# Float32 score and fold products as 64x32 tiles on a pair of PSUM banks, two conversion steps on GpSimd

## Chip, core and metric

The kernel runs on one core of a Trainium2 chip. The metric is the device time of one execution in microseconds (us), lower is better. PE is TensorE (PEld its weight loads), DVE is VectorE, ACT is ScalarE, POOL is GpSimd; SP only issues transfers. A matmul multiplies a stationary operand (`lhsT`, up to 128 rows by 128 columns) with a moving one (`rhs`) into PSUM, which has eight banks of 512 float32 columns in each of 128 partitions. A product that uses only 64 or 32 of the stationary columns writes only as many partitions, and another product can use the other columns at the same time. A float32 product stands in the profile as two MATMUL rows, a float16 product as one.

## What is computed

Eight batches of eight heads: attention over 32 memory slots that are made from k, v and phi, and then a feed-forward layer on all 4608 tokens, with g = h cos(h).

```python
def _attn_ref(q, k, v, phi):
    a = np.exp(phi - np.max(phi, axis=2, keepdims=True))
    a = a / (np.sum(a, axis=2, keepdims=True) + 1e-09)
    k_m = np.einsum('bhsm,bhsd->bhmd', a, k)
    v_m = np.einsum('bhsm,bhsd->bhmd', a, v)
    scores = scale * np.matmul(q, k_m.transpose(0, 1, 3, 2))
    attn = np.exp(scores - np.max(scores, axis=-1, keepdims=True))
    attn = attn / (np.sum(attn, axis=-1, keepdims=True) + 1e-09)
    return np.matmul(attn, v_m)

h = x @ w_in          # x: (4608, 512), the attention's output; w_in: (512, 2048)
g = h * np.cos(h)
return g @ w_out      # w_out: (2048, 512)
```

The shapes are 8 batches, 8 heads, 576 positions, head size 64, 32 slots. The weights arrive as 64-bit floats.

## The kernel before

**Folding.** The attention's last product and the layer's first are both linear, so the kernel multiplies v_m with w_in once for each batch (the *fold*, 256 x 2048) and then takes h as attn times the fold. Batch 0 folds in float32 (`fold_first`, eight pieces of 256 columns), batch 1 in float32 as well (`fold`, four pieces q of 512 columns); batches 2 to 7 fold in float16 pairs, a high and a low part.

**Groups.** The 4608 tokens are taken as 12 groups of 384. A group has 16 steps f, one for each 128 of the 2048 hidden columns: `gemm1` makes h (tile `hp`), `act` and `act_end` make g on ACT and DVE, `gemm2` adds g times w_out to three accumulators (`acc`), four steps behind. Group 0 works in float32, the others in float16 pairs. Step f of `gemm2` reads `wo[:, f + 1]`.

**Conversion.** w_in comes in eight pieces (in0 to in7), w_out in eight (out0 to out7), each as 1024 pairs of 32-bit words in every partition. `to_float32` makes float32 of them: DVE writes the sign into the upper 16 bits (line 143), ACT writes the first bits below it (147), ACT scales the high words in place (151), DVE joins them (152), ACT squares for the later scale (154). The pieces follow in the order out0, in2, in3, out1, out2, in4, in5, out3, out4, in6, in7, out5, out6, out7, one in each step of group 0 (`convert_next`); in0 and in1 come ahead of it. Piece out j becomes `wo[2j+1]` and `wo[2j+2]`, so step f = 12 needs out6 and f = 14 needs out7. Raw words lie in three rotating buffers (`raw0` to `raw2`), in2 and in3 in free parts of `wo`; the next load into a buffer waits for the square. When in7 and out7 are done, `weight_scale` takes a maximum over all partitions with a GpSimd all-reduce (line 178), and all float16 parts of the weights need its result.

**Attention of a batch.** `memory` makes k_m and v_m (`psA`, then a transposing product into `tpx`), and copies them into `km` and `vm`, 64 columns for a pair of heads: the two heads lie in the two halves of the rows and of the columns, and GpSimd sets the rest to zero. Another all-reduce (line 312) gives v's scale. `attend` makes the scores in blocks of 256, 256 and 64 positions, transposes them on DVE in 32 x 32 squares, takes the softmax and transposes back. It is a generator, 24 steps long, that the main loop runs a few steps at a time beside the groups of the batches ahead of it.

**Order.** Each engine has one queue, worked off in order. A scheduler sets the order from the written one; the line behind a wait waits too. Scores, folds and other small products share two PSUM banks that rotate (`small_ps`).

Of the kernel before, what the change touches and what calls it, by code (L numbers as in the profile page):

```python
# [45 lines left out]
def attention_then_ffn(ctx: ExitStack, tc: tile.TileContext, phi, phiT, kv, qT, w_in, w_out, eye, out):  # L46
# [86 lines left out]

    def to_float32(dst, raw, sq_to, pin=False, after_sign=None):
# [8 lines left out]
        sign = nc.vector.tensor_scalar(out=halves[:, :, :, 1], in0=high_top, scalar1=0.0, scalar2=-32768.0,  # L143
                                       op0=ALU.is_lt, op1=ALU.mult)
# [2 lines left out]
        begin = nc.scalar.activation(halves[:, :, :, 0], low_top, AF.Copy, scale=2.0 ** -5, bias=-31.0 / 64.0)
# [3 lines left out]
        nc.scalar.activation(high.bitcast(F32), high.bitcast(F32), AF.Copy, scale=2.0 ** -112)
        nc.vector.scalar_tensor_tensor(out=dst.bitcast(I32), in0=high, scalar=3, in1=dst.bitcast(I32),
                                       op0=ALU.logical_shift_left, op1=ALU.bitwise_or)
        nc.scalar.activation(low.bitcast(F32), dst, AF.Square, accum_out=sq_to)

    def convert_w_in(j, after_sign=None):
        to_float32(w_in_sb[:, :, j * WS:(j + 1) * WS], loads.pop(("in", j)), sq[:, 0, j:j + 1], j == 1, after_sign)

# [68 lines left out]
    def memory(b):  # L227
# [65 lines left out]
        km = wk.tile([P, NP, 2 * M], F32, tag="km", name=f"km_{b}", bufs=1)
        vm = wk.tile([P, NP, 2 * M], F32, tag="vm", name=f"vm_{b}")
        nc.gpsimd.memset(km, 0.0)
        nc.gpsimd.memset(vm, 0.0)
# [52 lines left out]
    def attend(b):  # L349
# [18 lines left out]

        sc_at = {}

        def score_products(i):
            t0, n = BL[i]
            sc_at[i] = sc = small_ps(f"sc_{b}_{t0}")
            for g in range(2):
                for p in range(2):
                    nc.tensor.matmul(sc[D * p:D * (p + 1), g * n:(g + 1) * n], lhsT=km[:, 2 * g + p],  # L376
                                     rhs=qt[:, 2 * g + p, t0:t0 + n], start=True, stop=True)
# [37 lines left out]
        if b == 0:  # L415
            for p in ((0, 1), (2,)):
                for i in p:
                    scores(i)
                if p[0] == 0:
# [9 lines left out]
        score_products(0)
        score_products(1)  # L430
        score_back(0)
        score_back(1)
# [27 lines left out]
    def fold_psum(b, q, g):  # L460
        pv = small_ps(f"pv_{b}_{q}_{g}")
        for i in range(2):
            c = 2 * g + i
            if b < 2:
                nc.tensor.matmul(pv[D * i:D * (i + 1)], lhsT=st["vm", b][:, c],
                                 rhs=w_in_sb[:, c, q * FS:(q + 1) * FS], start=True, stop=True)
        if b >= 2:
            for first in (True, False):
                for j in range(4):
                    c, o = 2 * g + j // 2, 1 - j % 2  # L470
                    nc.tensor.matmul(pv[M * j:M * (j + 1)], lhsT=(st["vp", b] if first else vl)[:, c, o],  # L471
                                     rhs=st["w2", q][:, c, o], start=first, stop=not first, skip_group_check=True)
# [8 lines left out]
    def fold(b, q):  # L481
        vw = wk.tile([P, 2, 2, FS], F16, tag="vw", name=f"vw_{b}_{q}", bufs=8)
        st["vw", b, q] = vw
        for g, pv in enumerate([fold_psum(b, q, g) for g in range(2)]):
            split_fold(b, vw, g, pv)

    def fold_first(j):
        q, r = divmod(j, 2)
# [2 lines left out]
        pv = small_ps(f"pvf_{j}").rearrange("p (g x) -> p g x", g=2)
        for g in range(2):
            for i in range(2):
                c = 2 * g + i
                nc.tensor.matmul(pv[D * i:D * (i + 1), g], lhsT=st["vm", 0][:, c],
                                 rhs=w_in_sb[:, c, j * WS:(j + 1) * WS], start=True, stop=True)
# [299 lines left out]
```

## Time and profile before

| what | value |
|---|---|
| median of 2 runs | 709.72 us (709.52 to 709.92) |
| the profiled execution | 710.08 us, its span 708.3 us |
| busy: PE, DVE, ACT, POOL | 97%, 75%, 73%, 2% of the span |
| first product of group 0's `gemm2` | at 41.6 us |
| group 1 opens (first L577) | at 125.2 us |
| mean granted TensorE clock | 0.994 of full speed |

Busy time of PE is that of its rows, which are pipelined, so a busy PE need not be PE at its peak. Releasers (behind `<-`) are inferred from semaphores.

```profile
PE   8699899999999999999999999999999999999997
DVE  3889879999968966599667886599567976575552
ACT  1899999897985865778666875778766875665652
POOL 0000000000000000000000100000000000000000
DMA  8996782326407100160105200160100000100101
PE acc L577 33%; PE hp L533 16%; DVE u L547 4%; ACT u L552 3%; DVE u L556 3%; DVE gp L559 3%; PE psA L270 3%; DVE vw L478 2%; PE sc L376 2%; PE pv L471 2%; ACT gp L558 2%; DMA phi<-in_phi 2%; DVE wo L191 2%; PE hp L524 1%; DVE w_in_parts L202 1%
```

The first five lines cut the span into 40 slices of 17.7 us; a digit is the busy share in tenths. The last line is the chain of work that ended last, its share of the span by line: half of it is the two large products, L577 and L533.

### The profile page before, as it was taken

The page shows a single profiled execution, that of the slowest core. Times are in us where ns is not written, and L with a number is a line of the kernel's source. Part 1 is how long each engine was busy: PE and PEld are TensorE (multiplying, and loading weights), DVE is VectorE, ACT ScalarE, POOL GpSimd, SP SyncE. Part 2 cuts the span into 40 slices and gives each one's busy share as a digit, 9 for nine tenths or more (in the row PEclk, how much of TensorE's full clock was granted, in tenths as well). Part 3 has the DMA queues.
Part 4 walks back from the last instruction along what each step waited for, and adds up shares of the span by engine and source line. Part 5 has one row for each costly group of instructions (what it writes and reads, how often), then busy time and mean ns, then how long its engine had stood idle before and what let it go on. Part 6 is the DMA issues. An engine that isn't in the chain of part 4 may idle for free.

```text
span 708.3 us, 11822 instructions
## 1 busy us (share of the span) xinstructions
PE 687.8 (97%) x4597; PEld 364.7 (51%) x4597; DVE 532.7 (75%) x1135; ACT 518.7 (73%) x951; POOL 13.7 (2%) x34
## 2 busy tenths in 40 slices
PE   8699899999999999999999999999999999999997
PEld 3354345565555445666445445666445454665553
DVE  3889879999968966599667886599567976575552
ACT  1899999897985865778666875778766875665652
POOL 0000000000000000000000100000000000000000
PEclk9999999999999999999999999999999999999999
DMA  8996782326407100160105200160100000100101
GB/s 281 379 321 218 266 293 60 105 61 195 146 1 237 44 1 1 56 226 1 44 1 167 99 16 1 46 206 31 44 2 2 22 23 1 46 1 1 45 1 44
DMA packets 31959, 66.18 MB, mean 93 GB/s; under 512 B 2208, under 2 KB 12320, under 8 KB 31904
## 3 DMA queue, kind: packets, MB, share of 16 engines
q1 hardware_dynamic: 27440, 57.43, 25.0%
q10 hardware_dynamic: 4464, 8.00, 3.0%
q8 instruction: 36, 0.59, 0.3%
q14 instruction: 19, 0.16, 0.1%
HBM read 51.79 MB, written 9.44 MB: 86 GB/s over the span
## 4 chain that ended last, share of the span: by engine, by line
PE 60%; DVE 21%; ACT 16%; DMA 2%; issue 1%; ACTq 0%; POOL 0%; DVEq 0%; SPq 0%
PE acc L577 33%; PE hp L533 16%; DVE u L547 4%; ACT u L552 3%; DVE u L556 3%; DVE gp L559 3%; PE psA L270 3%; DVE vw L478 2%; PE sc L376 2%; PE pv L471 2%; ACT gp L558 2%; DMA phi<-in_phi 2%; DVE wo L191 2%; PE hp L524 1%; DVE w_in_parts L202 1%
## 5 line engine op out<-in xcount | busy, mean ns | idle before, releaser
L577 PE MATMUL acc<-wo,gp 128*128 128x512 f16 x1584 | 371.8, 379 | 1.2 <-DVE ob L589 0.7
L577 PEld LDWEIGHTS <-gp 128*128 128x128 f16 x1584 | 153.3, 98 | 162.6 <-issue 4.1
L533 PE MATMUL hp<-aT,vw 128*128 128x192 f16 (+1 forms) x1440 | 202.7, 284 | 1.0 <-DVE u L556 1.0
L533 PEld LDWEIGHTS <-vw 128*128 128x128 f16 x1440 | 128.3, 98 | 77.4 <-issue 17.5
L552 ACT ACTIVATE u<-u,quarter 128x384 f32<-128x384 f32 x192 | 116.7, 615 | 63.8 <-DVE u L547 62.9
L556 DVE SCALAR_TENSOR_TENSOR u<-hp,u 128x384 f32<-128x384 f32 x176 | 96.5, 553 | 60.6 <-ACT u L552 60.1
L544 ACT ACTIVATE gp<-hp,cu 128x192 int32<-128x192 f32 (+1 forms) x240 | 115.4, 492 | 28.1 <-PE hp L533 12.3
L547 DVE SCALAR_TENSOR_TENSOR u<-hp,cu,gp 128x192 f32<-128x192 f32 (+1 forms) x240 | 118.8, 503 | 21.9 <-ACT gp L544 21.5
L559 DVE TENSOR_TENSOR gp<-u,gp 128x384 f16<-128x384 f32 x176 | 96.4, 552 | 43.0 <-ACT gp L558 41.9
L558 ACT CAST gp<-u 128x384 f16<-128x384 f32 x176 | 88.8, 510 | 54.3 <-DVE u L556 53.0
L572 PE MATMUL acc<-wo,gp 128*128 128x512 f32 x96 | 45.1, 599 | 0.0
L478 DVE SCALAR_TENSOR_TENSOR vw<-pv,vw 128x512 f16<-128x512 f32 x48 | 31.5, 684 | 3.0 <-ACT vw L477 2.9
L524 PE MATMUL hp<-aT,vf 128*128 128x384 f32 x64 | 25.6, 533 | 7.9 <-DVE vf L497 3.1
L477 ACT ACTIVATE vw<-pv 128x512 f16<-128x512 f32 x48 | 26.8, 589 | 1.1 <-PE pv L471 0.9
L572 PEld LDWEIGHTS acc<-wo,gp 128*128 128x128 f32 x96 | 17.4, 190 | 17.8 <-issue 15.2
L601 ACT ACTIVATE ob<-acc,os 128x512 f32<-128x512 f32 x27 | 17.8, 682 | 9.6 <-PE acc L577 7.1
L524 PEld LDWEIGHTS hp<-aT,vf 128*128 128x128 f32 x64 | 12.2, 202 | 20.1 <-issue 4.3
L552 ACT ACT_TABLE_LOAD x17 | 21.8, 1283 | 0.3
L270 PE MATMUL psA<-kv,phi 128*32 128x129 f32 (+1 forms) x640 | 21.0, 275 | 0.7 <-ACT phi L260 0.5
L376 PE MATMUL sc<-q,km 128*64 128x256 f32 (+3 forms) x192 | 19.8, 342 | 1.6 <-DVE vw L478 1.2
L270 PEld LDWEIGHTS psA<-kv,phi 128*32 128x32 f32 (+1 forms) x640 | 16.4, 109 | 7.3 <-issue 3.3
L376 PEld LDWEIGHTS sc<-q,km 128*64 128x64 f32 x192 | 12.1, 140 | 12.0 <-issue 3.6
(136 smaller groups left out, 544.7 us busy)
## 6 DMA issues: line engine op xcount, KB each, us to landing
kv<-in_kv SPq DMA_DIRECT2D x32, 516.0 KB, 6.9
raw_out<-in_w_out SPq DMA_DIRECT2D x8, 1024.0 KB, 5.8
q<-in_qT SPq DMA_DIRECT2D x7, 1152.0 KB, 6.0
out<-ob ACTq DMA_DIRECT2D x30, 256.0 KB, 2.1
raw_in<-in_w_in SPq DMA_DIRECT2D x6, 1024.0 KB, 8.1
phi<-in_phi SPq DMA_DIRECT2D x8, 512.0 KB, 5.9
w_in_sb<-w_in_parts SPq DMA_DIRECT2D x12, 256.0 KB, 4.0
kv<-in_kv SPq DMA_DIRECT2D x8, 258.0 KB, 8.5
```

The lines of the kernel that those rows point to most:

```text
L270: nc.tensor.matmul(psA[32 * j:32 * (j + 1), g * KV:(g + 1) * KV], lhsT=a[:n, c, h * M:(h + 1) * M], rhs=kvs[c][:n, h * KV:(h + 1) * KV], s ...
L376: nc.tensor.matmul(sc[D * p:D * (p + 1), g * n:(g + 1) * n], lhsT=km[:, 2 * g + p], rhs=qt[:, 2 * g + p, t0:t0 + n], start=True, stop=True)
L478: nc.vector.scalar_tensor_tensor(out=vw[:, 1, g], in0=src, scalar=T, in1=vw[:, 0, g], op0=ALU.mult, op1=ALU.subtract)
L533: nc.tensor.matmul(hp[:, c0:c0 + n], lhsT=vw[:, wi, g, fo * P:(fo + 1) * P], rhs=aT[:, ai, g, c1:c1 + n], start=(k == 0), stop=(k == 5))
L544: ins = nc.scalar.activation(ni[:, c], hp[:, c], AF.Copy, scale=cu, bias=0.25)
L547: nc.vector.scalar_tensor_tensor(out=u[:, c], in0=hp[:, c], scalar=cu, in1=ni[:, c], op0=ALU.mult, op1=ALU.subtract)
L552: nc.scalar.activation(u, u, AF.Sin, scale=TWO_PI_BELOW, bias=quarter)
L556: nc.vector.scalar_tensor_tensor(out=u, in0=hp[:, :GT], scalar=2.0 ** -17, in1=u, op0=ALU.mult, op1=ALU.mult)
L558: nc.scalar.copy(gp[:, 0], u)
L559: nc.vector.tensor_tensor(out=gp[:, 1], in0=u, in1=gp[:, 0], op=ALU.subtract)
L572: nc.tensor.matmul(accs[grp][t], lhsT=gp[:, t * P:(t + 1) * P], rhs=wo[:, f + 1], start=(f == 0), stop=(f == NF - 1))
L577: nc.tensor.matmul(accs[grp][t], lhsT=gp[:, gi, t * P:(t + 1) * P], rhs=parts[:, wi], start=(f == 0 and gi == 0 and wi == 0), stop=(f == N ...
```

## The change

**Tiles.** `km` and `vm` lose their zero halves: 32 columns for a pair of heads, the even head's 64 rows over the odd head's (for `vm` the other way round). A score product now takes 64 rows and 32 columns, one head, and the head's half g goes to bank g of a pair of banks; column quarter c takes pair c. A block is eight products. The float32 folds are cut the same way (`fold_single`); the float16 folds keep their shape. Scores come in two blocks of 288 positions instead of 256, 256 and 64 (batch 0: 384 and 192). The two banks that rotated are now one tile, `pair`, whose halves are handed out in turn.

**Conversion.** For all pieces but in0 and in1 the sign goes from DVE to GpSimd and the scaling from ACT to GpSimd. Each is a TENSOR_SCALAR over 1024 columns. GpSimd's memsets of `km` and `vm` are gone.

```diff
@@ attention_then_ffn
+    ps_s = ctx.enter_context(tc.tile_pool(name="ps_s", bufs=1, space=PSUM))
+    pair = ps_s.tile([P, 2, 512], F32, name="pair")
+    turn = itertools.count()
     def small_ps(name):
-        return ps_s.tile([P, 512], F32, tag="ps_s", name=name)
+        return pair[:, next(turn) % 2]
@@ to_float32
-        sign = nc.vector.tensor_scalar(out=halves[:, :, :, 1], in0=high_top, scalar1=0.0, scalar2=-32768.0,
-                                       op0=ALU.is_lt, op1=ALU.mult)
+        sign = (nc.vector if early else nc.gpsimd).tensor_scalar(out=halves[:, :, :, 1], in0=high_top, scalar1=0.0, scalar2=-32768.0,
+                                                                        op0=ALU.is_lt, op1=ALU.mult)
...
-        nc.scalar.activation(high.bitcast(F32), high.bitcast(F32), AF.Copy, scale=2.0 ** -112)
+        if early:
+            nc.scalar.activation(high.bitcast(F32), high.bitcast(F32), AF.Copy, scale=2.0 ** -112)
+        else:
+            nc.gpsimd.tensor_scalar(out=high.bitcast(F32), in0=high.bitcast(F32), scalar1=2.0 ** -112, scalar2=None,
+                                    op0=ALU.mult)
@@ memory
-        nc.gpsimd.memset(km, 0.0)
-        nc.gpsimd.memset(vm, 0.0)
...
-        nc.scalar.mul(km[lo, :, 0:M], tv[lo, :, 0], 1.0 / math.sqrt(D))
+        nc.scalar.mul(km[lo], tv[lo, :, 0], 1.0 / math.sqrt(D))
@@ attend
         def score_products(i):
             t0, n = BL[i]
-            sc_at[i] = sc = small_ps(f"sc_{b}_{t0}")
-            for g in range(2):
-                for p in range(2):
-                    nc.tensor.matmul(sc[D * p:D * (p + 1), g * n:(g + 1) * n], lhsT=km[:, 2 * g + p],
-                                     rhs=qt[:, 2 * g + p, t0:t0 + n], start=True, stop=True)
+            for c in range(NP):
+                for g in range(2):
+                    rows = slice(g * D, (g + 1) * D)
+                    nc.tensor.matmul(pair[M * c:M * (c + 1), g, :n], lhsT=km[rows, c],
+                                     rhs=qt[rows, c, t0:t0 + n], start=True, stop=True)
 
         def score_back(i):
             t0, n = BL[i]
-            nc.vector.transpose(at[:, 2 * t0:2 * (t0 + n)], sc_at[i][:, :2 * n])
+            for g in range(2):
+                nc.vector.transpose(at[:, 2 * t0 + g * n:2 * t0 + (g + 1) * n], pair[:, g, :n])
@@ after fold_psum
+    def fold_single(b, c0, n):
+        for c in range(NP):
+            for g in range(2):
+                rows = slice((1 - g) * D, (2 - g) * D)
+                nc.tensor.matmul(pair[M * c:M * (c + 1), g, :n], lhsT=st["vm", b][rows, c],
+                                 rhs=w_in_sb[rows, c, c0:c0 + n], start=True, stop=True)
```

Lines of the changed program are numbered anew: the sign is line 145, the scaling 156, the joining 158, scores 378, the all-reduces 184, 229 and 316.

POOL's queue up to the third batch, before (an ISA row with a name is an all-reduce, one without a name has no operands and stands ahead of an instruction of another kind; `km` and `vm` are set to zero):

```order
L296 MEMSET vm_480 128x256
L312 ISA
L312 ISA l_0_235<-l_0_233 128x1
L295 MEMSET km_479 128x256
L312 ISA l_1_492<-l_1_490 128x1
L295 MEMSET km_1587 128x256
L296 MEMSET vm_1588 128x256
L178 ISA m_in<-m_in 128x1
L178 ISA m_out<-m_out 128x1
```

The same queue now, from out2 to in5's scaling (`raw_out_324` is out2, `raw_in_328` and `raw_in_344` are in4 and in5, `l_1` is v's scale of batch 1):

```order
L145 TENSOR_SCALAR wo<-raw_out_324 128x1024
L156 TENSOR_SCALAR raw_out_324<-raw_out_324 128x1024
L316 ISA
L316 ISA l_1_494<-l_1_492 128x1
L145 ISA
L145 TENSOR_SCALAR w_in_sb<-raw_in_328 128x4x256
L145 TENSOR_SCALAR w_in_sb<-raw_in_344 128x4x256
L156 TENSOR_SCALAR raw_in_328<-raw_in_328 128x1024
L156 TENSOR_SCALAR raw_in_344<-raw_in_344 128x1024
```

The memsets are gone, two TENSOR_SCALAR rows stand for each piece, and a row without operands stands wherever the queue goes between an all-reduce and a TENSOR_SCALAR.

The end of the conversions on the same queue now (`raw_out_588` is out5, `raw_out_625` out6, `raw_out_648` out7):

```order
L156 TENSOR_SCALAR raw_out_588<-raw_out_588 128x1024
L184 ISA
L184 ISA m_in<-m_in 128x1
L145 ISA
L145 TENSOR_SCALAR wo<-raw_out_625 128x1024
L145 TENSOR_SCALAR wo<-raw_out_648 128x1024
L156 TENSOR_SCALAR raw_out_625<-raw_out_625 128x1024
L156 TENSOR_SCALAR raw_out_648<-raw_out_648 128x1024
L184 ISA
L184 ISA m_out<-m_out 128x1
```

The all-reduce for w_in's scale now stands between out5 and out6, and both signs stand ahead of both scalings.

PE's queue at the scores of batch 4, before (`sc_0` and `sc_256` are its first two blocks, `gp_4` is step 4 of a group) and then now:

```order
L577 MATMUL acc_0_2923<-wo,gp_4_2914 128x512
L376 MATMUL sc_0_3139<-q_2223,km_3062 64x256 x4
L376 MATMUL sc_256_3144<-q_2223,km_3062 64x256 x4
L577 LDWEIGHTS gp_4_2914
L577 MATMUL acc_0_2923<-wo,gp_4_2914 128x512
```

```order
L572 MATMUL acc_0_2915<-wo,gp_5_2981 128x512
L378 MATMUL pair<-q_2229,km_3052 32x288 x8
L572 LDWEIGHTS gp_5_2981
L572 MATMUL acc_0_2915<-wo,gp_5_2981 128x512
L572 LDWEIGHTS gp_5_2981
```

Eight products of 64 rows, 32 columns and 288 positions stand where eight of 128 rows, 64 columns and 256 positions stood; the second block of eight follows some rows later, where the third block of four small products stood.

More of the change, by code (lines that the diff above doesn't have):

```diff
@@ L156, in convert_w_in @@
     def convert_w_in(j, after_sign=None):
[L157 removed]
+        to_float32(w_in_sb[:, :, j * WS:(j + 1) * WS], loads.pop(("in", j)), sq[:, 0, j:j + 1], j == 1, after_sign, j < 2)
     def convert_w_out(j):
@@ L292, in memory @@
             nc.tensor.matmul(tpx[:, g * P:(g + 1) * P], lhsT=X[:, g], rhs=ident, start=True, stop=True)
[L293 to L296, printed above, removed]
+        km = wk.tile([P, NP, M], F32, tag="km", name=f"km_{b}", bufs=1)
+        vm = wk.tile([P, NP, M], F32, tag="vm", name=f"vm_{b}")
         tv = tpx[:, 0:HM].rearrange("p (c t m) -> p c t m", t=2, m=M)
         lo, hi = slice(0, D), slice(D, P)
-        nc.scalar.mul(km[lo, :, 0:M], tv[lo, :, 0], 1.0 / math.sqrt(D))
-        nc.scalar.mul(km[hi, :, M:2 * M], tv[hi, :, 1], 1.0 / math.sqrt(D))
-        nc.vector.tensor_copy(out=vm[hi, :, 0:M], in_=tv[hi, :, 0])
-        nc.vector.tensor_copy(out=vm[lo, :, M:2 * M], in_=tv[lo, :, 1])
+        nc.scalar.mul(km[lo], tv[lo, :, 0], 1.0 / math.sqrt(D))
+        nc.scalar.mul(km[hi], tv[hi, :, 1], 1.0 / math.sqrt(D))
+        nc.vector.tensor_copy(out=vm[hi], in_=tv[hi, :, 0])
+        nc.vector.tensor_copy(out=vm[lo], in_=tv[lo, :, 1])
         st["km", b], st["vm", b] = km, vm
@@ L415, in attend @@
         if b == 0:
[L416 to L419, printed above, removed]
+            for i in range(2):
+                p = (i,)
+                scores(i)
+                if i == 0:
                     yield
@@ L424, in attend @@
                 normalize(p)
-                for i in p:
-                    back(i)
+                back(i)
                 yield
             return
[L429 to L432, printed above, removed]
+        scores(0)
         yield
-        score_products(2)
-        score_back(2)
+        scores(1)
         yield
@@ L438, in attend @@
             load_q(b + 1)
-        pieces = ((0,), (1, 2))
+        pieces = ((0,), (1,))
         for p in pieces:
@@ L453, in attend @@
         yield
+        yield
         back(1)
         yield
-        back(2)
-        yield
     def fold_psum(b, q, g):
[L461 to L472, printed above, removed]
-        return pv
+        pv = pair[:, g]
+        for first in (True, False):
+            for c in range(NP):
+                nc.tensor.matmul(pv[M * c:M * (c + 1)], lhsT=(st["vp", b] if first else vl)[:, c, 1 - g],
+                                 rhs=st["w2", q][:, c, 1 - g], start=first, stop=not first, skip_group_check=True)
+        return pv
+    def fold_single(b, c0, n):
+        for c in range(NP):
+            for g in range(2):
+                rows = slice((1 - g) * D, (2 - g) * D)
+                nc.tensor.matmul(pair[M * c:M * (c + 1), g, :n], lhsT=st["vm", b][rows, c],
+                                 rhs=w_in_sb[rows, c, c0:c0 + n], start=True, stop=True)
     def split_fold(b, vw, g, src):
@@ L483, in fold @@
         st["vw", b, q] = vw
-        for g, pv in enumerate([fold_psum(b, q, g) for g in range(2)]):
-            split_fold(b, vw, g, pv)
+        if b < 2:
+            fold_single(b, q * FS, FS)
+        for g in range(2):
+            split_fold(b, vw, g, fold_psum(b, q, g) if b >= 2 else pair[:, g])
     def fold_first(j):
@@ L490, in fold_first @@
             st["vf", q] = wk.tile([P, 2, FS], F32, tag="vw", name=f"vf_{q}", bufs=8)
[L491 to L496, printed above, removed]
+        fold_single(0, j * WS, WS)
+        pv = pair[:, :, 0:WS]
         (nc.scalar.copy if j < 2 else nc.any.tensor_copy)(out=st["vf", q][:, :, r * WS:(r + 1) * WS], in_=pv)
```

10 lines of the change are left out of this document (4 added, 6 removed).

## The prediction

> **What bounds the kernel now.** I read the busy sums of six stretches first, to learn which engine is full where.
>
> ```profile
> 20.00:41.60 21.60, 14.63 (x63) 6.85 (x61) 16.96 (x24) 20.09 (x27) 0.00 (x0) 0.92 1.05 359
> 41.60:83.40 41.80, 38.66 (x207) 19.25 (x206) 38.08 (x75) 39.27 (x57) 0.98 (x3) 0.96 0.77 267
> 83.40:125.20 41.80, 41.80 (x169) 20.58 (x168) 36.71 (x82) 41.60 (x71) 1.02 (x3) 1.00 0.56 178
> 183.40:708.30 524.90, 518.25 (x3588) 276.89 (x3585) 376.05 (x805) 362.21 (x693) 9.38 (x17) 1.00 0.15 50
> ```
>
> The columns are length, then busy time of PE, PEld, DVE, ACT and POOL, the granted clock, DMA share and GB/s. From 183 us on PE is busy for 518.25 of 524.90 us: there the end moves by what PE is relieved of. Until 125 us, where group 0 runs and the weights are converted, ACT is full (41.60 of 41.80), and POOL does next to nothing (1.02). Second, the timeline of the stretch in which conversion ends, to see what waits for it.
>
> ```profile
> 97.42 2.74 PE L572 MATMUL acc<-wo,gp 128*128 128x512 f32 x6
> 100.00 1.45 PE L524 MATMUL hp<-aT,vf 128*128 128x384 f32 x4
> 101.28 2.74 PE L572 MATMUL acc<-wo,gp 128*128 128x512 f32 x6
> 108.86 2.77 PE L572 MATMUL acc<-wo,gp 128*128 128x512 f32 x6
> 111.56 1.94 PE L465 MATMUL pv<-w_in_sb,vm 128*64 128x512 f32 x8
> 125.21 0.81 PE L577 MATMUL acc<-wo,gp 128*128 128x512 f16 x3
> ...
> 97.91 1.23 DVE L152 SCALAR_TENSOR_TENSOR wo<-raw_out,wo 128x1024 int32<-128x1024 int32 x1 [0.46 <-ACT raw_out L151]
> 104.05 1.23 DVE L152 SCALAR_TENSOR_TENSOR wo<-raw_out,wo 128x1024 int32<-128x1024 int32 x1 [0.21 <-ACT raw_out L151]
> ```
>
> The L572 rows at 97.42, 101.28 and 108.86 are f = 9, 10 and 12 of group 0; L577 at 125.21 opens group 1. Step f = 12 reads what out6 became, and that was ready at 99.14 (97.91 + 1.23), out7 at 105.28. So conversion now leads its reader by about 10 us.
>
> **The change, part by part.** *Conversion.* Fourteen of the sixteen conversions (all but in0 and in1) hand the sign to POOL instead of DVE, and the scaling to POOL instead of ACT.
>
> ```profile
> L143 DVE TENSOR_SCALAR wo<-raw_out 128x1024 int16<-128x1024 int8 x8 | 6.0, 751 | 0.0
> L151 ACT ACTIVATE raw_out<-raw_out 128x1024 f32<-128x1024 f32 x8 | 9.2, 1147 | 0.0
> L154 ACT ACTIVATE raw_out<-wo 128x1024 f32<-128x1024 f32 x8 | 9.3, 1161 | 0.0
> L223 POOL PARTITION_ALL_REDUCE mx<-mx x4 | 5.1, 1278 | 22.9 <-DVE mx L222 11.8 <-DVE rs L395 11.1
> L296 POOL MEMSET vm<- 128x256 f32 x8 | 2.4, 312 | 134.8 <-DVE vl L343 53.6 <-PE pv L465 36.3 <-PE pvf L495 31.2
> 222.34 1.07 POOL L223 PARTITION_ALL_REDUCE mx<-mx  x1 [4.73 <-DVE mx L222]
> ```
>
> Off DVE go 14 x 0.75 = 10.5 us, off ACT 14 x 1.15 = 16.1 us. On POOL come 28 instructions over 1024 columns, and the trace has none like them. The lower end is the memset, which only writes: 0.312 us for 256 columns, at most 1.25 us for 1024. The upper end is the all-reduce, which reads, computes and writes 256 columns: 1.07 us in a single row, 1.28 in the mean of four, so 4.3 to 5.1 us for 1024. A scaling reads, computes and writes, and the sign does two operations and writes 2-byte pieces 4 bytes apart: I hold them nearest to the all-reduce and take 4.7 us, 9.4 us for a conversion. Conversions now come every 5.2 us (83.6 us of group 0 in 16 steps), so POOL becomes the engine on which group 0 waits, and what DVE and ACT save buys nothing.
>
> *Code on POOL.* In the changed program's POOL order, five unnamed ISA rows stand ahead of out6: each time POOL goes between the all-reduce and TENSOR_SCALAR. Before, that row stands once, ahead of the first all-reduce, and the profile knows it by another name:
>
> ```profile
> L312 POOLq MODIFY_POOL_CONFIG  x2: 13/13/13, 1.6 to 1.6; - x2
> 17.30 0.35 POOL L312 PARTITION_ALL_REDUCE l<-l  x1 [15.76 <-DVE l L310]
> L552 ACT ACT_TABLE_LOAD x17 | 21.8, 1283 | 0.3
> ```
>
> Issued at 1.6, first used at 17.30: such a switch of code costs between nothing and 15.7 us. ACT's table load, 1.28 us, is the only other row in which an engine changes what it runs, and it fetches a table, not code; no row settles it, so I take the middle of the ends, 7.8. The Trainium skill (GPSIMD Engine Reference, Instruction dispatch) gives about 6 us for the first call after such a load, which no run here shows yet; by it the five come to 30 us in place of 39, and my time would be 9 us lower.
>
> *The sum on POOL.* POOL is free at 17.65 (17.30 + 0.35). Ahead of out6's last scaling lie 12 conversions and three of the four instructions of out6 and out7 (both signs stand first): 13.5 x 9.4 = 126.9 us. Add five switches, 39.0, and two all-reduces, 0.7.
>
> One stall comes on top. Out1's scaling waits for ACT's first step on out1, and that stands on ACT behind in3's square, which waits through DVE for POOL's scaling of in3.
>
> ```profile
> 41.26 1.13 ACT L154 ACTIVATE wo<-w_in_sb 128x1024 f32<-128x1024 f32 x1
> 49.86 1.39 ACT L147 ACTIVATE wo<-raw_out 128x1024 int16<-128x1024 uint8 x1
> ```
>
> From the square's end (42.39) to that step ACT needs 7.5 us; with the step itself 8.9. Ahead go DVE's 1.23 and the square's 1.13, and POOL covers 4.7 with out1's sign: 11.3 - 4.7, some 6.6 us of stall. Then DVE's last step on out6, 1.2. In all 17.65 + 126.9 + 39.0 + 0.7 + 6.6 + 1.2 = 192.1 us, where step f = 12 could start at 108.86: 83.2 us later. Two things could come later still, and don't.
>
> ```profile
> 107.23 0.35 POOL L178 PARTITION_ALL_REDUCE m_out<-m_out  x1 [14.07 <-DVE m_out L177]
> 111.59 0.77 ACT L190 ACTIVATE wo<-wo,s_out 128x512 f16<-128x512 f32 x1
> ...
> raw_out<-in_w_out SPq DMA_DIRECT2D x8, 1024.0 KB, 5.8
> ```
>
> Group 1 also needs w_out's scale: out7's scaling, a sixth switch, the all-reduce and the 4.0 us that now lie between it and the first split (107.58 to 111.59) make 4.7 + 7.8 + 0.4 + 4.0 = 16.9 us behind out6's last scaling; step 12's own way to group 1 takes 1.2 + 16.4 (125.21 - 108.86). And three raw buffers rotate, so a load has about two conversions, 19 us, against 5.8 us to landing.
>
> *Scores.* Six batches (2 to 7) have theirs in the part that PE bounds.
>
> ```profile
> 308.07 1.95 PE L376 MATMUL sc<-q,km 128*64 128x256 f32 x16
> 309.95 1.90 PE L577 MATMUL acc<-wo,gp 128*128 128x512 f16 x8
> 311.78 0.45 PE L376 MATMUL sc<-q,km 128*64 128x64 f32 x8
> 312.16 1.17 PE L533 MATMUL hp<-aT,vw 128*128 128x192 f16 x12
> ...
> 48.19 2.54 PE L270 MATMUL psA<-kv,phi 128*32 128x129 f32 x80
> ```
>
> PE goes on 1.88 us after the first, 0.38 after the second: 2.26 a batch. The 16 rows (a float32 product is two) went in pairs on two halves of the columns, 1.88 / 8 = 0.235 us for a pair of 256 columns, 0.264 at 288. That column quarters run four at a time L270 shows: 80 rows of 129 columns in fours, at 0.235 x 129 / 256, make 2.4 us, against 2.54 seen. Whether row halves also run together no row shows. If they do, a block of 16 rows takes two rounds, 0.53 us, a batch 1.06, and six batches save 7.2 us. At four together a batch takes 2.1 and nothing is saved; at two, 4.2, and 12 us are lost. I take eight, since the streams into the array (eight of 64 rows) are as many as L270's four of 128.
>
> *Folds in float32.* Batch 1's second to fourth fold lie behind step f = 12 or beside it. One takes 1.94 us (x8 at 111.56); at twice the products together half is saved, 3 x 0.97 = 2.9 us. Batch 0's eight lie in the shadow of POOL's queue.
>
> *At nothing.* Two banks as one tile: a product pair waits for both banks to be read, and PE's steps between two scores or folds cover that. Transposes: four of 288 columns for 512, 512 and 64 a batch, on DVE, which has 149 us free behind 183 us. The memsets leave POOL, 16 x 0.31 us that nobody waited for.
>
> **Sum.** The profiled execution took 710.08 us, with its span 708.3 (its idle ends make 1.8), and lies 0.36 above the median of 709.72. 710.1 + 83.2 - 7.2 - 2.9 = 783.2.
>
> **Rivals.** *POOL at two passes of the memset.* If an instruction reads and writes at the memset's pace, it takes 2 x 1.0 us (three memsets start 0.25 us apart), a conversion 4.1. POOL ends late when 5 switches + 13.5 conversions pass 89.3 us (108.86 - 17.65 - 1.2 - 0.7): at 4.1 and 6.8 us just not. With 7.8 and the stall: 5 + 6.6 us later, less 10.1, about 712 us: no change.
>
> ```profile
> 0.73 0.31 POOL L295 MEMSET km<- 128x256 f32 x1 [0.29 <-POOLq L784]
> 0.98 0.56 POOL L296 MEMSET vm<- 128x256 f32 x2
> ```
>
> For it: the memset's rows. Against it: the only POOL row that computes is four times as slow. The Trainium skill (GPSIMD Engine Reference, Elementwise) stands with this rival: 1.8 to 2.6 cycles an element at 1.2 GHz, by my estimate 1.5 to 2.2 us for 1024; the all-reduce's row does not agree, and no run here shows the instruction itself.
>
> *POOL as cheap as the memset, switches as a table load.* Then 13.5 x 2.5 + 5 x 1.3 = 40 us: conversion is never late, ACT's relief counts. Group 0's PE rows make 16 x (2.58 + 1.28) = 61.8 of its 83.6 us, and ACT sheds 14 of its 81; I give it half of that, 7. Scores 7.2, batch 1's four folds 3.9: 710.1 - 18.1 = 692 us, faster. For it speaks that POOL is empty now.
>
> *DVE and POOL in each other's way.* If a DVE instruction with two operands in SBUF and POOL's reads exclude each other, POOL waits for fourteen of 1.23 us and for some 5 us of batch 1's, about 22 us: 805. No row here shows POOL reading beside DVE. The Trainium skill (SBUF, Who interferes with whom) states such an exclusion.
>
> **How the numbers follow.** Forecast 783: 0.66. DVE in the way, 805: 0.11. Two passes, 712: 0.13. Cheap, 692: 0.10. So slower by over 2% 0.77, within 2% (about what a measurement of this kernel tells from no change) 0.13, faster 0.10. The forecast's own range: with 4.3 us, 1.3 us and no stall 733; with 5.1 and 7.8 794; with switches at 15.7 823. From the slow end the range must reach into the second rival to leave out 2 in 10: 705 to 820.
>
> **What would show it.** POOL busy for about 130 us until some 200 us, with TENSOR_SCALAR rows of 4 to 5 us; L158 on DVE released by POOL; group 1 opening near 205 us. Rows of 2 us or less, or group 1 opening near 120, and the forecast is wrong. Scores: L378's 16 rows over about 0.55 us if eight run together, 1.05 if four. Gaps of 5 to 15 us between an all-reduce and the next TENSOR_SCALAR tell the switch's price.

## The result and the profile after

The changed kernel takes 767.06 us (median of 2 runs, 765.90 to 768.22) against 709.72: a ratio of 1.081 (95% interval 1.074 to 1.088), slower. The profiled execution took 765.9 us, its span is 764.1. The forecast was 783 us, in a range of 705 to 820.

The page's slices of the changed kernel, 19.1 us each, show where the time came in; then three windows (length, busy time of PE, PEld, DVE, ACT and POOL, granted clock, DMA share, GB/s).

```profile
PE   8679177479998999999999999999999999999997
ACT  2559164469998777668776777576866696675652
POOL 0692897420000000000000000000000000000000
PEclk9879689779999999999999999999999999999999
```

```profile
41.60:83.40 41.80, 31.80 (x224) 14.27 (x222) 32.15 (x63) 27.87 (x41) 23.12 (x8) 0.91 0.60 218
83.40:125.20 41.80, 21.09 (x99) 8.94 (x100) 17.94 (x17) 17.81 (x28) 41.47 (x13) 0.73 0.40 132
174.60:764.10 589.50, 574.28 (x4086) 299.21 (x4084) 433.97 (x921) 420.51 (x794) 6.43 (x10) 1.00 0.18 58
```

POOL is full where ACT was full before: 41.47 of 41.80 us, with PE down from 41.80 to 21.09, ACT from 41.60 to 17.81, and the granted clock at 0.73. The timeline of PE shows the last and decisive wait:

```profile
157.22 4.64 PE L567 MATMUL acc<-wo,gp 128*128 128x512 f32 x6 [12.13 <-DVE wo L158]
161.79 1.08 PE L469 MATMUL pair<-w_in_sb,vm 64*32 64x512 f32 x14
163.81 2.77 PE L567 MATMUL acc<-wo,gp 128*128 128x512 f32 x6
167.40 2.77 PE L567 MATMUL acc<-wo,gp 128*128 128x512 f32 x6
171.00 2.77 PE L567 MATMUL acc<-wo,gp 128*128 128x512 f32 x6
174.59 2.11 PE L572 MATMUL acc<-wo,gp 128*128 128x512 f16 x9
```

L567 at 157.22 is step f = 12, which reads what out6 became. It stands 48.4 us later than before (108.86), and group 1 opens 49.4 us later (174.59 against 125.21). Behind that the program took 589.5 us against 583.1 (708.3 - 125.2): 6.4 us more, where the forecast had some 9 less (its 10.1 include a fold, about 1 us, that lay ahead of the opening, at 111.56). 49.4 + 6.4 make the 55.8 us between the two spans.

Step f = 12 was not the only place where PE waited for DVE's join. The list of waits (total us, times, longest) has more of it at batch 0's float32 folds, which need the pieces of w_in one by one:

```profile
PE pair L469 <- DVE w_in_sb L158: 21.9, 5, 14.0
PE acc L567 <- DVE wo L158: 12.1, 1, 12.1
```

In the kernel before, those folds waited 2.1 us for it. And after its wait step f = 12 itself was slow: its six rows took 4.64 us for 2.77, at a granted clock of 0.60 (157.2 to 161.8).

POOL's own timeline, the rows beside its pauses:

```profile
17.54 0.35 POOL L316 PARTITION_ALL_REDUCE l<-l  x1 [17.11 <-DVE l L314]
25.89 4.02 POOL L145 TENSOR_SCALAR wo<-raw_out 128x1024 int16<-128x1024 int8 x1 [8.00 <-DMA raw_out<-in_w_out]
30.00 3.26 POOL L156 TENSOR_SCALAR raw_out<-raw_out 128x1024 f32<-128x1024 f32 x1
...
51.22 2.91 POOL L156 TENSOR_SCALAR raw_out<-raw_out 128x1024 f32<-128x1024 f32 x1
...
68.52 0.38 POOL L316 PARTITION_ALL_REDUCE l<-l  x1 [7.38 <-DVE l L314]
79.94 7.91 POOL L145 TENSOR_SCALAR w_in_sb<-raw_in 128x1024 int16<-128x1024 int8 x2 [11.05 <-issue]
...
136.54 0.38 POOL L184 PARTITION_ALL_REDUCE m_in<-m_in  x1 [8.21 <-ACT u L547]
144.32 7.92 POOL L145 TENSOR_SCALAR wo<-raw_out 128x1024 int16<-128x1024 int8 x2 [7.40 <-issue]
152.19 5.70 POOL L156 TENSOR_SCALAR raw_out<-raw_out 128x1024 f32<-128x1024 f32 x2
163.54 0.38 POOL L184 PARTITION_ALL_REDUCE m_out<-m_out  x1 [5.66 <-DVE w_in_parts L208]
```

At each change between all-reduce and TENSOR_SCALAR stands a pause of 5.7 to 11.05 us; between two TENSOR_SCALARs there is none. Not every pause is the price of the change. The 8.00 ended with out0's load, and the 7.38 ended 0.14 us after DVE had made what the all-reduce reads (L314, done at 68.38). Of the 5.66, the first 2.7 passed before its operand was made (L183, done at 160.63). The 8.21 is clean, since its operand was made at 125.01, before the pause began; ahead of the 11.05 and the 7.40 the profile shows nothing that was waited for. The groups of POOL up to 175 us give the rows' price (count, busy us, mean ns, idle before):

```profile
L145 POOL TENSOR_SCALAR wo<-raw_out 128x1024 int16<-128x1024 int8 x8 | 31.9, 3992 | 15.4 <-DMA raw_out<-in_w_out 8.0 <-issue 7.4
L156 POOL TENSOR_SCALAR raw_out<-raw_out 128x1024 f32<-128x1024 f32 x8 | 23.6, 2952 | 0.5
L145 POOL TENSOR_SCALAR w_in_sb<-raw_in 128x1024 int16<-128x1024 int8 x4 | 16.0, 4005 | 11.0 <-issue 11.0
L156 POOL TENSOR_SCALAR raw_in<-raw_in 128x1024 f32<-128x1024 f32 x4 | 11.5, 2895 | 0.2
```

A sign takes 4.0 us, a scaling 2.9 (two more groups, on `wo`, are alike); a conversion is 6.95 us of POOL. The view of the sign's line has one row more that bears on the pauses:

```profile
L145 POOLq MODIFY_POOL_CONFIG  x6: 83/83/83, 17.8 to 136.9; - x6
```

Two such rows come ahead of each first sign behind an all-reduce, the first at 17.8 us, right at the all-reduce's end (17.54 + 0.35), 8 us ahead of the sign, and so with the last (136.9, sign at 144.32). I read the pause as POOL changing its code; no row shows what it does in it.

### The profile page after: what moved, and what is told of

It reads as the page before. It is cut to its first block, busy times and chain, and to the rows that moved or that the text cites. A ratio compares the mean times of both kernels' runs of the same rounds, so it can differ in the third digit from the quotient of the medians.

```text
span 764.1 us, 12127 instructions
## 1 busy us (share of the span) xinstructions
PE 692.2 (91%) x4757; PEld 351.8 (46%) x4757; DVE 535.0 (70%) x1112; ACT 512.4 (67%) x935; POOL 104.5 (14%) x46
## 4 chain that ended last, share of the span: by engine, by line
PE 37%; DVE 17%; issue 15%; ACT 15%; POOL 9%; DMA 4%; SPq 1%; DVEq 0%; POOLq 0%; ACTq 0%
PE acc L572 18%; PE hp L528 11%; ACT u L547 4%; DVE gp L554 3%; DVE u L542 3%; DVE u L551 3%; ACT gp L553 3%; PE pair L572 3%; POOL w_in_sb L145 3%; POOL wo L145 3%; PE acc L567 2%; PE pair L461 2%; DMA raw_out<-in_w_out 2%; POOL raw_out L156 2%; ACT gp L539 2%
## 5 line engine op out<-in xcount | busy, mean ns | idle before, releaser
L572 PE MATMUL acc<-wo,gp 128*128 128x512 f16 x1488 | 355.9, 379 | 0.4 <-ACT ob L596 0.4
L572 PEld LDWEIGHTS <-gp 128*128 128x128 f16 x1584 | 151.6, 98 | 167.8 <-issue 14.9
L567 PE MATMUL acc<-wo,gp 128*128 128x512 f32 x96 | 48.6, 642 | 16.4 <-DVE wo L158 12.1
L316 POOL PARTITION_ALL_REDUCE l<-l x8 | 2.8, 356 | 430.2 <-DVE l L314 430.2
L475 DVE SCALAR_TENSOR_TENSOR vw<-pair,vw 128x512 f16<-128x512 f32 x48 | 33.1, 690 | 10.8 <-ACT vw L474 10.1
L519 PE MATMUL hp<-aT,vf 128*128 128x384 f32 x64 | 31.0, 628 | 7.6 <-DVE aT L409 4.1
L567 PEld LDWEIGHTS acc<-wo,gp 128*128 128x128 f32 x96 | 18.9, 206 | 38.8 <-issue 17.8
L469 PE MATMUL pair<-w_in_sb,vm 64*32 64x256 f32 (+1 forms) x192 | 12.6, 523 | 25.3 <-DVE w_in_sb L158 21.9
L145 POOL TENSOR_SCALAR wo<-raw_out 128x1024 int16<-128x1024 int8 x8 | 31.9, 3992 | 15.4 <-DMA raw_out<-in_w_out 8.0
L474 ACT ACTIVATE vw<-pair 128x512 f16<-128x512 f32 x48 | 28.3, 589 | 7.4 <-PE pair L461 7.2
L158 DVE SCALAR_TENSOR_TENSOR wo<-raw_out,wo 128x1024 int32<-128x1024 int32 x8 | 13.3, 1668 | 22.6 <-POOL raw_out L156 21.8
L160 ACT ACTIVATE raw_out<-wo 128x1024 f32<-128x1024 f32 x8 | 9.1, 1136 | 24.9 <-DVE wo L158 24.8
```

What stands on the lines that cost most here:

```text
L145: sign = (nc.vector if early else nc.gpsimd).tensor_scalar(out=halves[:, :, :, 1], in0=high_top, scalar1=0.0, scalar2=-32768.0, op0=ALU.is ...
L475: nc.vector.scalar_tensor_tensor(out=vw[:, 1, g], in0=src, scalar=T, in1=vw[:, 0, g], op0=ALU.mult, op1=ALU.subtract)
L519: nc.tensor.matmul(hp[:, :GT], lhsT=st["vf", q][:, g, fo * P:(fo + 1) * P], rhs=st["aTf"][:, g], start=(g == 0), stop=(g == 1))
L567: nc.tensor.matmul(accs[grp][t], lhsT=gp[:, t * P:(t + 1) * P], rhs=wo[:, f + 1], start=(f == 0), stop=(f == NF - 1))
L572: nc.tensor.matmul(accs[grp][t], lhsT=gp[:, gi, t * P:(t + 1) * P], rhs=parts[:, wi], start=(f == 0 and gi == 0 and wi == 0), stop=(f == N ...
```

## The experiments

Theory 1: POOL's queue, rows and code changes together, makes the whole delay of group 1's opening, and the tiles cost some 6 us behind it. All twelve kernels in one table, with before and after; "opens" is the first row of group 1's second product, "behind" the rest of the span.

| kernel | median us | ratio to before (95%) | opens at | behind |
|---|---|---|---|---|
| before | 709.72 | | 125.2 | 583.1 |
| after | 767.06 | 1.081 (1.074 to 1.088) | 174.6 | 589.5 |
| e1 tiles alone | 715.70 | 1.009 (1.008 to 1.011) | 123.6 | 590.3 |
| e2 conversion alone | 756.99 | 1.067 (1.066 to 1.069) | 170.9 | 583.9 |
| e3 sign alone | 736.89 | 1.039 (1.037 to 1.040) | 144.1 | 590.2 |
| e4 scaling alone | 737.58 | 1.040 (1.039 to 1.042) | 152.7 | 582.8 |
| e5 after, folds first | 763.17 | 1.075 (1.073 to 1.077) | 173.4 | 586.0 |
| e6 e1, folds first | 715.12 | 1.007 (1.006 to 1.009) | 123.6 | 588.3 |
| e7 e6, two tiles | 716.70 | 1.011 (1.009 to 1.012) | 129.9 | 584.2 |
| e8 after, no all-reduce | 741.19 | 1.045 (1.043 to 1.047) | 150.0 | 588.1 |
| e9 scores alone | 713.96 | 1.008 (1.005 to 1.010) | 127.7 | 584.6 |
| e10 e8, one all-reduce | 754.20 | 1.063 (1.061 to 1.065) | 163.6 | 588.8 |
| e11 e4, no all-reduce | 725.28 | 1.023 (1.021 to 1.024) | 140.1 | 584.0 |
| e12 after, two multiplies | 752.09 | 1.059 (1.056 to 1.062) | 160.9 | 589.3 |

**Which half of the change costs: e1 and e2.** In e1 every conversion has `early=True`; e2 is the kernel before with the two GpSimd instructions of `to_float32`.

```diff
-        to_float32(w_in_sb[:, :, j * WS:(j + 1) * WS], loads.pop(("in", j)), sq[:, 0, j:j + 1], j == 1, after_sign, j < 2)
+        to_float32(w_in_sb[:, :, j * WS:(j + 1) * WS], loads.pop(("in", j)), sq[:, 0, j:j + 1], j == 1, after_sign, True)
```

> All sixteen conversions stay on VectorE and ScalarE, the rest is the changed kernel: 64x32 products, the pair of banks, blocks of 288. Theory 1 (GpSimd's queue makes the whole delay of group 1's opening, 174.6 against 125.2 us, and the 64x32 tiles make what lies behind it longer by 6.4 us, 589.5 against 583.1): group 1 opens near 125 us, the time is 716 us (710 to 720), slower than before by about 1%. Rival 1 (the prediction's gain of 10 us in scores and folds is there, and something of GpSimd's conversions costs the 16 us behind group 1's opening): 700 us. Rival 2 (sharing one pair of banks also delays group 0): group 1 opens at 130 us or later, 722 us or more.

> The kernel before, with nothing changed but sign and scaling of conversions 3 to 16 on GpSimd. Theory 1 (the queue on GpSimd is the whole delay): 25.9 us at the first sign, 12 conversions of 6.95 us and two pairs of code changes of about 18.8 and 16 us ahead of out6's sign, as in the changed kernel; group 1 opens near 174 us, behind it the 583 us of the kernel before: 759 us (755 to 763), GpSimd busy about 115 us with the memsets. Rival 1 (conversion also costs behind group 1's opening): 766 to 776 us. Rival 2 (the pair of banks has a share in the 49 us): under 752 us.

715.7 and 757.0 us: theory 1 in both. The conversion costs 47 us, nearly all of it ahead of group 1 (which opens at 170.9 against 125.2; behind it 583.9 against 583.1). The tiles cost 6 us, all of it behind the opening (590.3 against 583.1). Alone, the two move the opening by +45.7 and -1.6 us, together by 49.4; the 5.3 us between arise only with both, and no run shows why.

**A queue, or a hand-over from step to step: e3 and e4.** The kernel before with one of the two instructions on GpSimd (the first piece of the diff is e3, the second e4).

```diff
-        sign = nc.vector.tensor_scalar(...
+        sign = (nc.vector if early else nc.gpsimd).tensor_scalar(...
...
-        nc.scalar.activation(high.bitcast(F32), high.bitcast(F32), AF.Copy, scale=2.0 ** -112)
...
+            nc.gpsimd.tensor_scalar(out=high.bitcast(F32), in0=high.bitcast(F32), scalar1=2.0 ** -112, scalar2=None,
+                                    op0=ALU.mult)
```

> The kernel before with only the sign on GpSimd (4.0 us a row), the scaling on ScalarE. Theory 1 (a queue: what counts is the sum on GpSimd against the 108.9 us at which out6 is needed): 25.9 + 12 x 4.05 + 18.8 + 16 + 4.05 = 113 us at the end of out6's sign, 2.5 us more through ScalarE and VectorE, so about 8 us late: 718 us (712 to 724). Rival (each conversion hands its own lengthening on: 14 x (4.0 - 0.75) = 45 us): about 755 us.

> The kernel before with only the scaling on GpSimd (2.9 us a row), the sign on VectorE. Theory 1 (a queue): 25.9 + 12 x 2.9 + 18.8 + 16 + 2.9 = 98 us at the end of out6's scaling, ahead of the 106 us at which it is needed: not late, 710 us (706 to 713), the same. Rival (each conversion hands on its lengthening, 14 x (2.9 - 1.14) = 25 us): about 735 us.

Both came out 27 us late. For the scaling alone theory 1 falls: 14 rows of 2.9 us and the changes of code don't fill POOL, and yet group 1 opens 27.5 us later; the rival's 735 is near. For the sign alone neither fits: its opening moves by 18.9 us (theory 1 had 8, the rival 45), and 7.1 us more arise behind it, 5.0 of them between the openings of groups 2 and 3 (60.0 us for 55.0); why is not settled. So a sum over POOL alone doesn't tell the delay. In e4 PE waits 20.7 us at batch 0's folds for pieces of w_in (2.1 before) and 5.0 at `gemm2` for pieces of w_out: single pieces came later than their readers, though POOL had time left in all.

**The changes of code by themselves: e8, e10, e11.** e8 leaves out the reductions over partitions ahead of group 1, which its result would need; e10 puts one back that no instruction reads; e11 does the same to e4 as e8 to the changed kernel.

```diff
-        nc.gpsimd.partition_all_reduce(m, m, channels=P, reduce_op=RED.max)
...
-        nc.gpsimd.partition_all_reduce(l3, l2, channels=P, reduce_op=RED.max)
+        l3 = l2
+        if b >= 2:
...
+            nc.gpsimd.partition_all_reduce(l3, l2, channels=P, reduce_op=RED.max)
...
+        if len(todo) == 9:
+            nc.gpsimd.partition_all_reduce(probe, sq[:, 1, 1:2], channels=P, reduce_op=RED.max)
```

> The changed kernel without the four all-reduces that GpSimd does ahead of group 1 (batch 0's and batch 1's maximum of v and the maxima of both weights): each partition then uses its own maximum. GpSimd's program has no change between all-reduce and TENSOR_SCALAR left ahead of group 1. Theory 1 (code changes are a good third of the queue: 8.0 + 18.8 + 16 us ahead of out6, 5.7 ahead of w_out's scale): the TENSOR_SCALAR rows stay at 4.0 and 2.9 us, 14 conversions take 97 us from about 20 us on, group 1 opens at 128 to 134 us and the time is 718 to 724 us. Rival (the rows and what they hand on from conversion to conversion make the delay, the changes hide beside waits for loads and VectorE): 740 us or more.

> The kernel without all-reduces ahead of group 1 (741.2 us), and one all-reduce of 128x1 put back in the middle of GpSimd's queue of conversions, whose result nobody reads. Theory 1 (each change of GpSimd between all-reduce and TENSOR_SCALAR costs some 7 us, whatever waits): a gap of 6 to 8 us ahead of the all-reduce and of 7 to 11 behind it, group 1 opens some 12 us later, 753 us (749 to 758). Rival (the gaps were waits for batch 1's and the weights' maxima): 0.4 us of work, 741 us.

> The kernel before with only the scaling on GpSimd, and without the four all-reduces ahead of group 1 (each partition then uses its own maximum). Theory 1 (of the 27.9 us that scaling alone costs, the code changes make nearly all, since 14 rows of 2.9 us fit beside the other work): group 1 opens at 125 to 129 us, 708 to 714 us. Rival (each conversion hands on the longer row, 14 x (2.9 - 1.14) = 25 us): 725 us or more.

e8's timeline of POOL, its first and last conversion, and e10's at the one all-reduce:

```profile
26.16 4.03 POOL L145 TENSOR_SCALAR wo<-raw_out 128x1024 int16<-128x1024 int8 x1 [25.73 <-DMA raw_out<-in_w_out]
...
124.18 2.94 POOL L156 TENSOR_SCALAR raw_out<-raw_out 128x1024 f32<-128x1024 f32 x1
```

```profile
59.40 2.98 POOL L156 TENSOR_SCALAR raw_out<-raw_out 128x1024 f32<-128x1024 f32 x1
68.56 0.38 POOL L693 PARTITION_ALL_REDUCE probe<-sq  x1 [6.18 <-ACT km L303]
78.52 4.02 POOL L145 TENSOR_SCALAR w_in_sb<-raw_in 128x1024 int16<-128x1024 int8 x1 [9.58 <-issue]
```

One all-reduce of 0.38 us that nobody waits for makes two pauses, 6.2 and 9.6 us, and 13.0 us on the time (754.2 - 741.2): theory 1 of e10. The second pause is clean, for the profile shows nothing that its sign waited for. The first is not: what the all-reduce reads, out1's square, was done only at 66.99, 4.6 us into it. Without any, POOL's conversions run from 26.16 to 127.12 almost without a pause, and group 1 opens 24.6 us earlier than in the changed kernel. By its expected times e8 still goes to the rival (740 us or more; theory 1 had 718 to 724), since it opens 24.8 us later than before. So the delay of 49.4 us halves: 24.6 go with the all-reduces and the pauses around them, 24.8 stay with the rows and what hangs on them. And the first pause was free: in e8 the first sign waits until 26.16 for out0's load, with no change of code ahead of it. In e11 group 1 still opens 14.9 us late, with POOL idle between its rows:

```profile
35.20 2.90 POOL L154 TENSOR_SCALAR wo<-wo 128x1024 f32<-128x1024 f32 x1 [3.62 <-DVE w_in_sb L143]
40.11 2.93 POOL L154 TENSOR_SCALAR wo<-wo 128x1024 f32<-128x1024 f32 x1 [2.01 <-DVE w_in_sb L143]
```

There the scaling waits for DVE's sign, and DVE's last step for the scaling: a hand-over, which the rival of e11 had (725 or more, measured 725.3). PE waits 13.2 us at batch 0's folds for pieces of w_in (2.1 before). Of the 27.9 us that scaling alone costs, 12.3 go with the changes of code.

**The tiles' 6 us: e5, e6, e7, e9.** The changed `fold` emits half, split, half, split; e5 and e6 emit both halves ahead of the splits. e7 has two rotating tiles in place of `pair`. In e9 folds and conversion are those of before; the folds keep the order of heads of before too, which changes what is multiplied but no instruction's size.

```diff
-        for g in range(2):
-            split_fold(b, vw, g, fold_psum(b, q, g) if b >= 2 else pair[:, g])
+        if b >= 2:
+            for g in range(2):
+                fold_psum(b, q, g)
+        for g in range(2):
+            split_fold(b, vw, g, pair[:, g])
```

```diff
-    ps_s = ctx.enter_context(tc.tile_pool(name="ps_s", bufs=1, space=PSUM))
-    pair = ps_s.tile([P, 2, 512], F32, name="pair")
+    ps_s = ctx.enter_context(tc.tile_pool(name="ps_s", bufs=2, space=PSUM))
...
+            sc_at[i] = sc = [small_ps(f"sc_{b}_{t0}_{g}") for g in range(2)]
```

> The changed kernel, but a float16 fold writes the products of both banks before the first split reads, as in the kernel before. Theory 1 (the changed program writes fold half, split, fold half, split; this cuts the 16 rows into two runs of 8 and makes PE wait for splits): the 24 folds go from 1.11 to 0.98 us, the extra 0.1 us in some 30 steps goes, and PE's waits at L461 (4.6 us) with it: 758 to 762 us against 767. Rival (the halves are harmless; the tiles cost where one pair of banks serves everything): 766 us or more.

> All conversions on VectorE and ScalarE, the 64x32 tiles, and both halves of a fold ahead of its splits. Theory 1: 715.7 us less the 5 to 9 us of the halves, 707 to 711 us, the same as before or a little faster. Rival (one pair of banks is the cost): 714 us or more.

> As the kernel with all conversions on VectorE and ScalarE and the folds' halves together, but the two banks are two tiles that rotate, as before, so that a product waits for its own bank alone; group 0's float32 folds are copied out by two instructions of 256 columns for one of 512. Theory 2 (the pair as one tile couples the banks and costs PE its waits): the scores' 5.8 us come out in full, 702 to 705 us, faster than the kernel with the pair. Theory 1 (only the halves cost): the same as with the pair, 707 to 711 us.

> The kernel before with the scores alone changed: 64x32 products on two rotating banks, blocks of 288 (384 and 192 in batch 0); conversion and all folds as before; one small buffer of row maxima less. Theory A (the 64x32 folds cost, in group 0 above all, and the scores' gain of 5.8 us comes out): 703 to 706 us. Theory B (the gain in scores is given back where it arises: the second block waits for the transposes of the first on both banks, and steps of VectorE and ScalarE end later): what lies behind group 2's opening stays 2 us longer than before, 709 to 713 us.

No theory came out as a whole. e5 (763.2) lies between its two; e6 (715.1) lies where its rival had it, yet e7, without the pair, is no faster (716.7) and outside both of its theories. In the profiled executions folds first takes 2.0 us off what lies behind group 1's opening in e6 (588.3 against e1's 590.3) and 3.5 in e5, but the intervals of e5 and the changed kernel overlap, and so do e6's and e1's. Two tiles take off 4.1 more (584.2; one execution of each, while e6's own runs lie up to 3.4 us apart). They lose it in group 0 (opening at 129.9), where a fold is copied out by two instructions and PE waits 7.2 us for a piece of w_out (2.8 in e6). e9 is nearest to theory B: behind group 2's opening it takes 527.1 us against 524.9, the 2 us that B had, but its time, 714.0, is 1 us above B's range. Windows from the opening to the end, of before, of e1 and of e7:

```profile
125.20:708.30 583.10, 575.20 (x4023) 309.86 (x4020) 433.01 (x929) 413.08 (x793) 10.36 (x20) 1.00 0.18 58
```

```profile
123.60:713.90 590.30, 575.99 (x4086) 299.99 (x4084) 433.98 (x924) 421.36 (x793) 6.41 (x10) 1.00 0.18 58
```

```profile
129.90:714.10 584.20, 571.97 (x4084) 303.43 (x4083) 428.98 (x915) 414.71 (x788) 7.30 (x10) 1.00 0.18 58
```

PE idles 7.9 us before (583.10 - 575.20), 14.3 in e1 and 12.2 in e7; its busy time falls by 3.2 us in e7, and by 4.3 at best (e5: 570.9 of 586.0). So part of the expected gain was given back as idle time. The waits are small and lie in other places in each kernel (e1: 1.6 us at L461 for splits, 1.4 at the scores for ACT; e7: 2.7 at the first product for DVE, 1.8 at the second for ACT). No run takes them all away; what makes them stays open.

**One or two operations on GpSimd: e12.**

```diff
-            nc.gpsimd.tensor_scalar(out=high.bitcast(F32), in0=high.bitcast(F32), scalar1=2.0 ** -112, scalar2=None,
-                                    op0=ALU.mult)
+            nc.gpsimd.tensor_scalar(out=high.bitcast(F32), in0=high.bitcast(F32), scalar1=2.0 ** -112, scalar2=1.0,
+                                    op0=ALU.mult, op1=ALU.mult)
```

> The changed kernel, with a second operation in GpSimd's scaling: multiply by 2 to the -112 and then by 1. Theory 1 (the sign's row is 1.1 us longer than the scaling's because it has two operations): the scaling's row goes from 2.9 to about 4.0 us, fourteen of them put 15 us more on the queue, some 12 us on the time: 779 us. Rival (the sign's bytes and halves, read and written 8 and 4 bytes apart, make its row longer, and a second operation is free): rows of 2.9 us, 767 us. Below that, rows well under 2.9 us would say that this form runs by another path: 750 us or less.

The third case, 2 us above the 750 that it had: 752.1 us, 15 less than the changed kernel. e12's groups on POOL up to 175 us:

```profile
L145 POOL TENSOR_SCALAR w_in_sb<-raw_in 128x1024 int16<-128x1024 int8 x4 | 16.0, 4017 | 12.6 <-DMA kv<-in_kv 12.6
L156 POOL TENSOR_SCALAR raw_out<-raw_out 128x1024 f32<-128x1024 f32 x8 | 9.5, 1192 | 0.5
```

A second multiplication cuts the scaling's row from 2.95 to 1.19 us. The fourteen rows lose 24.2 us (40.9 to 16.7), and group 1 opens 13.7 us earlier. The sign kept its 4.0 us, so the number of operations is not what makes it the longer row; why a second multiplication helps no run shows. None of the twelve kernels beats the kernel before.

## Why the forecast came out

**The mechanism was right, the closeness in part luck.** POOL's queue became what group 0 waits on, and group 1's late opening made 49.4 of the 55.8 us lost. But two larger errors cancelled in part. Counted from step f = 12, as the forecast counts, that step came 34.9 us earlier than foretold, and what lies behind it took 17.5 us more (606.9 us for 599.4 before, where 10.1 less were foretold); the sum is the 17 us between the forecast and the profiled execution. As foretold, L158 on DVE waits for POOL, POOL is busy for most of the stretch, and pauses of 5 to 15 us stand at the changes of code.

**Its terms.** Step f = 12 was set at 192.1 us and came at 157.22, 34.9 us earlier. POOL was free at 17.89 (17.65 foretold). From there:

| term | foretold | measured |
|---|---|---|
| rows ahead of out6's last scaling (14 signs, 13 scalings) | 126.9 | 94 |
| five changes of code | 39.0 | 42.0 (8.00 + 7.38 + 11.05 + 8.21 + 7.40) |
| stall at out1 | 6.6 | 0 |
| DVE's last step on out6 | 1.2 | 2.1 |

The rows were mis-sized: 4.7 us each, "nearest to the all-reduce", where a sign takes 4.0 and a scaling 2.9. The all-reduce's price per column was no measure of a TENSOR_SCALAR. The Trainium skill (GPSIMD Engine Reference, Elementwise) would have 1.5 to 2.2 us, an estimate from its 1.8 to 2.6 cycles an element. Of GpSimd's TENSOR_SCALAR rows here only two, e12's of 1.51 and 1.75, come near that band: 2.9 and 4.0 stand above it, the rest of e12's scalings, 1.1 to 1.2, below.

The stall doesn't exist, because its dependency doesn't: "Out1's scaling waits for ACT's first step on out1" is false. POOL scales out1 at 51.22 (above), and ACT's first step on it follows ten microseconds later:

```profile
61.75 1.38 ACT L149 ACTIVATE wo<-raw_out 128x1024 int16<-128x1024 uint8 x1
```

The five pauses at changes of code were set at the middle of two far ends, 7.8 us, and measured 8.4 on average; since no row had backed that middle, its closeness is luck. Two of the five were priced and cost nothing by themselves: without the change the 8.00 would still have waited for out0's load, which e8 shows landing as late, and the 7.38 for the operand of the all-reduce. The other three make 26.7 us, 8.9 each. The Trainium skill (GPSIMD Engine Reference, Instruction dispatch) has about 6 us for the first call to newly loaded code. The shortest pause of the changed kernel, 5.66, comes near to that; those ahead of a TENSOR_SCALAR that waited for nothing else, 7.40 and 11.05, don't.

And taking terms off the sum doesn't take as much off the time: removing the pauses behind the first (34.0 us; 39.7 with the sixth, ahead of w_out's all-reduce) moved the opening by 24.6, and cutting 24.2 us of rows moved it by 13.7. Other waits then end last; in e12, for one, POOL waits 3.1 us for a load that it had not waited for.

**Scores and folds.** Eight products do run together. PE's timeline at a batch's scores in the changed kernel:

```profile
364.25 0.72 PE L378 MATMUL pair<-q,km 64*32 64x288 f32 x16
364.90 1.47 PE L572 MATMUL acc<-wo,gp 128*128 128x512 f16 x6
366.67 0.72 PE L378 MATMUL pair<-q,km 64*32 64x288 f32 x16 [0.30 <-DVE at L384]
367.32 0.39 PE L572 MATMUL acc<-wo,gp 128*128 128x512 f16 x1
```

PE goes on 0.65 us after each block (0.53 foretold), 1.30 a batch for 2.26, so six batches save 5.8 us and not 7.2. A float32 fold's rows take 1.09 us for 1.94, 0.85 less (0.97 foretold). The step that failed is "at nothing": one tile for two banks, and new blocks, were held free because PE's steps between would cover the waits. PE's idle time behind the opening went from 7.9 to 15.2 us (589.50 - 574.28) and the float16 folds were cut in halves, and some 9 us less behind the opening became 6.4 more. By one execution each, e6 and e7 account for some 6 us of that difference (2.0 and 4.1); the rest stays open.

**The rivals.** Two memset passes and cheap POOL fall with the rows' price. DVE and POOL in each other's way: they are, but it is mostly DVE that pays. The changed kernel's L158, min/median/max in ns, against 1.23 us before:

```profile
L158 DVE SCALAR_TENSOR_TENSOR wo<-raw_out,wo x8: 1215/1658/2175, 33.3 to 157.9; 128x1024 int32<-128x1024 int32 x8
L158 DVE SCALAR_TENSOR_TENSOR w_in_sb<-raw_in,w_in_sb x6: 1212/2084/2096, 21.7 to 121.4; 128x1024 int32<-128x1024 int32 x6
```

The join, which has two operands in SBUF, takes 2.1 us where it starts within 0.1 us of the start of a POOL row, nine times of sixteen. It takes 1.22 with POOL idle, and also where it starts some 2 us into a POOL row (at 35.31 and 41.95). Nearly all of POOL's rows keep their 2.9 and 4.0; in e8 a scaling that starts while a join is running (at 65.68, the join from 65.42 to 66.64) takes 3.77. The Trainium skill (SBUF — State Buffer, Who interferes with whom) calls the ports that such a pair shares an exclusive lock. The 0.9 us by which the later one is longer may be such a wait; the two joins at full speed inside a POOL row don't agree with it. POOL did not wait for 22 us, so the rival's 805 us falls.

## What to carry to other kernels

An idle engine is no free engine: price its instruction in the very form that it will run, for here one and the same scaling took 2.95 us, or 1.19 with a second multiplication, by 1. On GpSimd, keep all-reduces out of a queue of ordinary instructions: one put in between cost 13 us, for 0.4 us of work, and the four of the changed kernel 26 (767.1 - 741.2). Putting them side by side might do as well; no run tried it. A step that is faster by itself (scores, 1.30 for 2.26 us a batch) gained nothing here, since PE waited more elsewhere, so look at the idle time of the bounding engine before and after, not at the step.

## What was not expected of the hardware

- A TENSOR_SCALAR with two multiplications on GpSimd, 1024 float32 a partition: 1.1 to 1.2 us in most rows. With one multiplication: 2.9 us.
- A single 0.38 us all-reduce between TENSOR_SCALARs: pauses of 6.2 us (4.6 of them ahead of its operand) and 9.6 us around it, 13.0 us on the kernel.
- Sixteen float32 rows of 64x32 products over 288 columns on two banks: 0.65 us, in two rounds of eight.
- A DVE instruction with two operands in SBUF: 2.1 us where it starts together with a GpSimd row, 1.22 with GpSimd idle or some 2 us into its row.
- The granted clock of TensorE fell to 0.73 where it waited most (83 to 125 us), against 1.00 in the same stretch before.
